# A grouped 1x1 convolution: 64 equal chunks, and seven stores of 120 and 8 rows

## The chip, the core and the metric

The kernel runs on one core of a Trainium2 chip. The metric is the device time of one execution in microseconds (us). Each core has a matrix engine (PE), a vector engine (DVE), a scalar engine (ACT), GpSimd (POOL), an engine that only issues and synchronises (SP), and sixteen DMA engines that carry all traffic between the chip's main memory (DRAM) and the core's two-dimensional memory of 128 rows, called partitions here as in the code.

## What is computed

A 1x1 convolution in 4 groups: each of 512 x 512 pixels has 192 channels, in four groups of 48, and each group is multiplied by its own 48 x 48 matrix. All of it is bf16, with sums in f32.

```python
B, H, W, C = x.shape          # 1, 512, 512, 192
xg = xp.reshape(B, H, W, G, Cg)          # G = 4, Cg = 48, k = 1: no padding
out = out + jnp.einsum('bhwgc,gcd->bhwgd', xg, w[0, 0])
return out.reshape(B, H, W, C)
```

So 262,144 pixels of 384 bytes are read and as many written: 100.7 MB each way.

## The kernel before

**Tiling.** The pixels are cut into chunks. A chunk of s pixels per partition is 128 x s consecutive pixels: partition p holds s of them, a contiguous run of s x 384 bytes in DRAM (`rows_view`, L102). `sizes` (L62) is the list of chunks: five of 4, 4, 8, 16 and 32 pixels (`HEAD`), sixty of 32 (`PPC`), and five of 32, 16, 8, 4 and 4 (`TAIL`), 70 in all. A chunk of 32 is 12,288 bytes a partition and 1.5 MB in all. There are five input buffers `x_sb` and five output buffers `o_sb` (`NB`); chunk n uses number n modulo 5.

**Work in a chunk.** Four pixels per partition make a group, 512 groups in all. For a group PE transposes six 128 x 128 pieces of `x_sb` into `xT_ps` (L181), DVE copies them to `xT_sb` (L235), and PE multiplies them in two rounds of three by a banded weight matrix `wt` into `o_ps` (L204). Two results of 128 x 384 f32 are then cast into `o_sb`: for seven groups in ten by ACT in one copy (L275), for the other three (`SHARE`) one by ACT (L272) and one by DVE (L242). PE's transposes run two groups ahead of its products (`LOOK`).

**Who issues what.** SP issues the loads in order (L149), the small load of the weights just behind the first chunk (L151). From the sixth chunk on, a load waits until PE has transposed the last group of the chunk that used the buffer. ACT issues the stores (L259) between its copies: the store of a chunk when the products of two further groups are done. ACT and DVE wait, before the first write into an output buffer, until the earlier store from it has landed (L242 and the copies at L272 and L275; the semaphores `st_sem`). Each transfer raises its semaphore by 16, by one for each DMA engine that has finished its share.

**PE's program.** `build_weights` (L160 to L169) puts the 48 x 48 matrices into the band by ten products and waits for the weights' load; then come the transposes of the first groups, the groups of `HEAD` one by one, a loop of 12 trips over five chunks of 32 each, and the groups of `TAIL`. Within the loop PE waits by taking from semaphores (`take`), in the tail by counting (`wq.wait`).

Of the kernel before, what the change touches and what calls it, by code (L numbers as in the profile page):

```python
# [11 lines left out]
C = GROUPS * CG  # L12
# [11 lines left out]

PPC = 32
NB = 5
HEAD = (4, 4, 8, 16, 32)
TAIL = (32, 16, 8, 4, 4)
NXP = 4
NOB = 4  # L30
NXS = 4
LOOK = 2
# [16 lines left out]
def shared(g):  # L49
    return (g % 10) in SHARE  # L50


def bass_standalone__grouped__vision_kernel(nc, x, w, out):
# [2 lines left out]
    npix = B * H * W_  # L56
    assert npix % 128 == 0
    per_part = npix // 128
    mid = per_part - sum(HEAD) - sum(TAIL)
    assert mid > 0 and mid % (NB * PPC) == 0  # L60
    n_mid = mid // PPC
    trips = n_mid // NB  # L62
    sizes = list(HEAD) + [PPC] * n_mid + list(TAIL)
    assert len(HEAD) % NB == 0
    n_chunks = len(sizes)

    xf = x.rearrange("b h w c -> (b h w) c")
    of = out.rearrange("b h w c -> (b h w) c")
# [7 lines left out]
    groups, g0 = [], []  # L76
# [2 lines left out]
        groups += [(n, lg) for lg in range(s // 4)]  # L79
    NG = len(groups)  # L80
    g1 = [g0[n] + sizes[n] // 4 for n in range(n_chunks)]
    L0 = g0[len(HEAD)]
    L1 = g0[len(HEAD) + n_mid]
    body = NB * PPC // 4
    assert body % NXP == 0 and body % 10 == 0 and (L1 - L0) == body * trips
    GT = L1

    dve_prog = []
    for g in range(NG + LOOK):
        if g < NG:  # L90
            dve_prog.append(("ev1", g))
        h = g - LOOK
# [3 lines left out]
    def actT_cnt(g):  # L96
        return g - GT + 1

    def dveT_cnt(g):
        return sum(1 for h in range(GT, g + 1) if shared(h))  # L100

    def rows_view(ap, n):  # L102
        s = sizes[n]
        return ap[pix0[n]:pix0[n] + 128 * s, :].rearrange("(p i) c -> p (i c)", p=128)

    with ExitStack() as es:
        block = es.enter_context(nc.Block())
        x_sb = [es.enter_context(nc.sbuf_tensor(f"x_sb{i}", [128, PPC * C], BF16)) for i in range(NB)]
        o_sb = [es.enter_context(nc.sbuf_tensor(f"o_sb{i}", [128, PPC * C], BF16)) for i in range(NB)]
# [8 lines left out]
        def sem(name):  # L118
            return es.enter_context(nc.semaphore(name))

        ld_sem = [sem(f"ld{i}") for i in range(NB)]
        st_sem = [sem(f"st{i}") for i in range(NB)]
# [3 lines left out]
        ev1_sem, ev2_sem, act_sem = sem("ev1_sem"), sem("ev2_sem"), sem("act_sem")  # L126
        ev2T_sem, actT_sem = sem("ev2T_sem"), sem("actT_sem")
# [14 lines left out]
        @block.sync  # L142
        def _(sp):
            wq = Waiter(sp)
            for n in range(n_chunks):
                b = n % NB
                if n >= NB:
                    wq.wait(t_done, g1[n - NB])
                sp.dma_start(x_sb[b][:, 0:sizes[n] * C], rows_view(xf, n)).then_inc(ld_sem[b], 16)  # L149
                if n == 0:  # L150
                    sp.dma_start(w_sb[:], wv).then_inc(w_sem, 16)  # L151

        @block.tensor
        def _(pe):
            wq = Waiter(pe)

            def take(s, v):
                pe.wait_ge(s, v).then_inc(s, -v)  # L158

            def build_weights():  # L160
                wq.wait(e_sem, 1)
                wq.wait(w_sem, 16)
                last = None
                for (tc, r, g, c0) in WBLOCKS:
                    s0 = ESHIFT - r
                    col = WOFF[tc] + c0
                    last = pe.matmul(o_ps[:, NOB - 1, col:col + CG], lhsT=esel[:, s0:s0 + 128],  # L167
                                     rhs=w_sb[:, g, :], start=True, stop=True, skip_group_check=True)
                last.then_inc(wb_sem, 1)  # L169

            def transposes(g):
                n, lg = groups[g]
                b = n % NB
                if g == 0:
                    wq.wait(id_sem, 1)
                if lg == 0:
                    take(ld_sem[b], 16)
                last = None
                for j in range(6):
                    col = lg * 2 * UC + j * 128  # L180
                    last = pe.transpose(xT_ps[:, g % NXP, j * 128:(j + 1) * 128],  # L181
                                        x_sb[b][:, col:col + 128], ident[:])
                last.then_inc(t_done, 1)

            def matmuls(g):
                xs = xT_sb[g % NXS]
                take(ev1_sem, 1)
                h = g - 2
                if h >= 0:
                    if h < GT:  # L190
                        take(act_sem, 1)
                        if shared(h):
                            take(ev2_sem, 1)
                    else:
                        wq.wait(actT_sem, actT_cnt(h))
                        if shared(h):
                            wq.wait(ev2T_sem, dveT_cnt(h))
                last = None
                for ul in range(2):
                    v = (2 * g + ul) % NOB  # L200
                    for tc in range(3):
                        j = ul * 3 + tc
                        c0, c1 = COLR[tc]
                        last = pe.matmul(o_ps[:, v, c0:c1], lhsT=xs[:, j * 128:(j + 1) * 128],  # L204
                                         rhs=wt[:, WOFF[tc]:WOFF[tc] + (c1 - c0)],
                                         start=(tc == 0), stop=(tc == 2), skip_group_check=True)
                last.then_inc(mm_done, 1)

            build_weights()
            for g in range(LOOK):  # L210
                transposes(g)
            pe.wait_ge(wc_sem, 1)
            for g in range(L0):
                transposes(g + LOOK)
                matmuls(g)
            with pe.Fori(0, trips):
                for g in range(L0, L0 + body):
                    transposes(g + LOOK)
                    matmuls(g)
            for g in range(L1, NG):  # L220
                if g + LOOK < NG:
                    transposes(g + LOOK)
                matmuls(g)

        @block.vector
        def _(dve):
            wq = Waiter(dve)
            wq.wait(wb_sem, 1)
            dve.tensor_copy(wt[:], o_ps[:, NOB - 1, 0:WCOLS]).then_inc(wc_sem, 1)  # L229
            waited_chunk = -1  # L230
            for (op, g) in dve_prog:
                n, lg = groups[g]
                if op == "ev1":
                    wq.wait(t_done, g + 1)
                    dve.tensor_copy(xT_sb[g % NXS][:], xT_ps[:, g % NXP, 0:2 * UC]).then_inc(ev1_sem, 1)  # L235
                else:
                    if waited_chunk != n:
                        waited_chunk = n
                        wq.wait(st_sem[n % NB], 16 * (n // NB))
                    wq.wait(mm_done, g + 1)  # L240
                    u = lg * 2 + 1
                    dve.tensor_copy(o_sb[n % NB][:, u * UC:(u + 1) * UC],  # L242
                                    o_ps[:, (2 * g + 1) % NOB, 0:UC]).then_inc(
                                        ev2_sem if g < GT else ev2T_sem, 1)

        @block.scalar
        def _(act):
            wq = Waiter(act)
            pending = []

            def store(n):
                b = n % NB
                g = g1[n] - 1
                if g < GT:
                    wq.wait(mm_done, g + 3)
                else:
                    wq.wait(actT_sem, actT_cnt(g))
                    wq.wait(ev2T_sem, dveT_cnt(g))
                act.dma_start(rows_view(of, n), o_sb[b][:, 0:sizes[n] * C]).then_inc(st_sem[b], 16)  # L259

            for g in range(NG):
                n, lg = groups[g]
                if lg == 0:
                    wq.wait(st_sem[n % NB], 16 * (n // NB))
                wq.wait(mm_done, g + 1)
                while pending and pending[0][1] <= g:
                    store(pending.pop(0)[0])
                v = (2 * g) % NOB
                ob = o_sb[n % NB]
                if shared(g):  # L270
                    u = lg * 2
                    ins = act.copy(ob[:, u * UC:(u + 1) * UC], o_ps[:, v, 0:UC])  # L272
                else:
                    dst = ob[:, lg * 2 * UC:(lg + 1) * 2 * UC].rearrange("p (u c) -> p u c", u=2)
                    ins = act.copy(dst, o_ps[:, v:v + 2, 0:UC])  # L275
                ins.then_inc(act_sem if g < GT else actT_sem, 1)
                if g == g1[n] - 1:
                    pending.append((n, g + 2 if g < GT else g + 1))
            for (n, _) in pending:
                store(n)  # L280
            for b in range(NB):
                act.wait_ge(st_sem[b], 16 * len(range(b, n_chunks, NB)))


# [26 lines left out]
```

## Time and profile before

| what | value |
|---|---|
| runs | 495.13, 495.61, 495.68 us, median 495.61 |
| the profiled execution's own time | 495.92 us |
| its span, first to last instruction | 493.8 us |
| PE clock granted, mean over the span | 0.986 |
| read from and written to DRAM | 100.68 and 100.66 MB, 408 GB/s over the span |
| one ACT copy of 768 columns (L275), of 384 (L272) | 799 ns x 359, 480 ns x 153 |
| one DVE copy of 768 columns (L235), of 384 (L242) | 554 ns x 512, 553 ns x 153 |
| one transposition, one product on PE (L181, L204) | 220 ns x 3072, 233 ns x 3072 |
| first loads of 192 KB, last stores of 192 KB, issue to landing (median) | 11.4, 7.3 us |
| SP's waits for PE's transposes, before loads | 438.7 us in 65 waits |

The profile's page divides the span by engine, DMA queue and line of the program. "Busy" is the time in which an engine carries out an instruction. The queue q1 carries SP's loads, q10 ACT's stores; their share is that of the time of all sixteen DMA engines, over the whole span. A table of stretches gives the same for any part of the span. In the table of waits a row says which engine waited at which line for which, in us, how often and at most how long. Matmuls are pipelined, so PE's mean times overlap.

### The profile page before, as it was taken

The page shows a single profiled execution, that of the slowest core. Times are in us where ns is not written, and L with a number is a line of the kernel's source. Part 1 is how long each engine was busy: PE and PEld are TensorE (multiplying, and loading weights), DVE is VectorE, ACT ScalarE, POOL GpSimd, SP SyncE. Part 2 cuts the span into 40 slices and gives each one's busy share as a digit, 9 for nine tenths or more (in the row PEclk, how much of TensorE's full clock was granted, in tenths as well). Part 3 has the DMA queues.
Part 4 walks back from the last instruction along what each step waited for, and adds up shares of the span by engine and source line. Part 5 has one row for each costly group of instructions (what it writes and reads, how often), then busy time and mean ns, then how long its engine had stood idle before and what let it go on. Part 6 is the DMA issues. An engine that isn't in the chain of part 4 may idle for free. (4 is left out here: it accounts for less than half of the span.)

```text
span 493.8 us, 15051 instructions
## 1 busy us (share of the span) xinstructions
PE 418.9 (85%) x6154; PEld 390.4 (79%) x6154; DVE 348.4 (71%) x666; ACT 349.7 (71%) x513; POOL 1.3 (0%) x8
## 2 busy tenths in 40 slices
PE   6987999999988888888888988888888888888962
PEld 5987899999878787787877877878778787787862
DVE  4776788888877776776776767677667767677750
ACT  3776788888867767677676766766767667676752
POOL 1000000000000000000000000000000000000000
PEclk9999999999999999999999999999999999999995
DMA  8999999999999999999999999999999999999663
GB/s 298 420 419 425 427 429 428 429 429 427 426 429 429 429 428 429 428 429 429 429 429 429 428 429 429 429 429 428 429 428 428 429 429 429 429 428 417 239 254 143
DMA packets 20386, 201.56 MB, mean 408 GB/s; under 512 B 2448, under 2 KB 3472, under 8 KB 4496
## 3 DMA queue, kind: packets, MB, share of 16 engines
q1 hardware_dynamic: 10288, 100.69, 48.4%
q10 hardware_dynamic: 10080, 100.67, 48.2%
q8 instruction: 7, 0.11, 0.1%
q14 instruction: 11, 0.09, 0.0%
HBM read 100.68 MB, written 100.66 MB: 408 GB/s over the span
## 5 line engine op out<-in xcount | busy, mean ns | idle before, releaser
L275 ACT CAST o_sb<-o_ps 128x768 bf16<-128x768 f32 x359 | 280.3, 799 | 103.6 <-PE o_ps L204 66.5
L235 DVE COPY xT_sb<-xT_ps 128x768 bf16<-128x768 bf16 x512 | 282.2, 554 | 97.2 <-PE xT_ps L181 92.6
L204 PE MATMUL o_ps<-wt,xT_sb 128*128 128x144 bf16 (+1 forms) x3072 | 298.0, 233 | 48.7 <-PEq L158 46.7
L181 PE MATMUL xT_ps<-ident,x_sb 128*128 128x128 bf16 x3072 | 257.0, 220 | 16.4 <-PEq L158 12.3
L204 PEld LDWEIGHTS o_ps<-wt,xT_sb 128*128 128x128 bf16 x3072 | 211.4, 98 | 67.0 <-issue 57.7
L181 PEld LDWEIGHTS xT_ps<-ident,x_sb 128*128 128x128 bf16 x3072 | 196.0, 98 | 26.2 <-issue 26.1
L242 DVE CAST o_sb<-o_ps 128x384 bf16<-128x384 f32 x153 | 84.6, 553 | 35.7 <-DMA out_dram<-o_sb 21.5
L272 ACT CAST o_sb<-o_ps 128x384 bf16<-128x384 f32 x153 | 73.4, 480 | 34.9 <-DMA out_dram<-o_sb 21.2
L229 DVE CAST wt<-o_ps 128x480 bf16<-128x480 f32 x1 | 0.7, 657 | 4.2 <-PE o_ps L167 4.2
L167 PE MATMUL o_ps<-w_sb,esel 48*128 48x48 bf16 x10 | 0.6, 209 | 3.6 <-DMA w_sb<-in_w_dram 3.6
L167 PEld LDWEIGHTS o_ps<-w_sb,esel 48*128 48x128 bf16 x10 | 0.5, 111 | 3.5 <-issue 3.5
L275 ACT ACT_TABLE_LOAD x1 | 1.3, 1283 | 0.8 <-PEq L296 0.8
L134 POOL TENSOR_SCALAR_AFFINE_SELECT esel<-esel 48x272 bf16<-48x272 bf16 x1 | 0.4, 406 | 0.0
L131 POOL MEMSET esel<- 48x272 bf16 x1 | 0.3, 318 | 0.3 <-POOLq L296 0.3
L138 POOL TENSOR_SCALAR_AFFINE_SELECT ident<-ident 128x128 bf16<-128x128 bf16 x1 | 0.3, 287 | 0.0
L132 POOL MEMSET ident<- 128x128 bf16 x1 | 0.2, 198 | 0.0
L296 POOL MEMSET const-bfloat16-1.0<- 128x1 bf16 x1 | 0.1, 102 | 0.0
L296 POOL MEMSET const-uint8-127<- 128x1 uint8 x1 | 0.1, 102 | 0.0
L296 POOL MEMSET const-float32-0.0<- 128x1 f32 x1 | 0.1, 99 | 0.3 <-issue 0.3
L296 POOL MEMSET const-float32-1.0<- 128x1 f32 x1 | 0.1, 99 | 0.0
## 6 DMA issues: line engine op xcount, KB each, us to landing
x_sb<-in_x_dram SPq DMA_DIRECT2D x62, 1536.0 KB, 30.9
out_dram<-o_sb ACTq DMA_DIRECT2D x62, 1536.0 KB, 30.5
x_sb<-in_x_dram SPq DMA_DIRECT2D x2, 768.0 KB, 17.8
out_dram<-o_sb ACTq DMA_DIRECT2D x2, 768.0 KB, 13.9
x_sb<-in_x_dram SPq DMA_DIRECT2D x4, 192.0 KB, 11.4
x_sb<-in_x_dram SPq DMA_DIRECT2D x2, 384.0 KB, 15.3
out_dram<-o_sb ACTq DMA_DIRECT2D x4, 192.0 KB, 7.3
out_dram<-o_sb ACTq DMA_DIRECT2D x2, 384.0 KB, 10.8
```

The source lines that it names most:

```text
L131: gp.memset(esel[:], 1.0).then_inc(p0_sem, 1)
L134: gp.affine_select(out=esel[:], in_=esel[:], pattern=[[-1, ECOLS]], compare_op=AluOpType.is_equal, fill=0.0, base=ESHIFT, channel_multipli ...
L138: gp.affine_select(out=ident[:], in_=ident[:], pattern=[[-1, 128]], compare_op=AluOpType.is_equal, fill=0.0, base=0, channel_multiplier=1) ...
L167: last = pe.matmul(o_ps[:, NOB - 1, col:col + CG], lhsT=esel[:, s0:s0 + 128], rhs=w_sb[:, g, :], start=True, stop=True, skip_group_check=True)
L181: last = pe.transpose(xT_ps[:, g % NXP, j * 128:(j + 1) * 128], x_sb[b][:, col:col + 128], ident[:])
L204: last = pe.matmul(o_ps[:, v, c0:c1], lhsT=xs[:, j * 128:(j + 1) * 128], rhs=wt[:, WOFF[tc]:WOFF[tc] + (c1 - c0)], start=(tc == 0), stop=( ...
L229: dve.tensor_copy(wt[:], o_ps[:, NOB - 1, 0:WCOLS]).then_inc(wc_sem, 1)
L235: dve.tensor_copy(xT_sb[g % NXS][:], xT_ps[:, g % NXP, 0:2 * UC]).then_inc(ev1_sem, 1)
L242: dve.tensor_copy(o_sb[n % NB][:, u * UC:(u + 1) * UC], o_ps[:, (2 * g + 1) % NOB, 0:UC]).then_inc(ev2_sem if g < GT else ev2T_sem, 1)
L272: ins = act.copy(ob[:, u * UC:(u + 1) * UC], o_ps[:, v, 0:UC])
L275: ins = act.copy(dst, o_ps[:, v:v + 2, 0:UC])
L296: nc = _bacc.Bacc("TRN2", target_bir_lowering=False, num_devices=1)
```

## The change

The head and the tail of small chunks go: all 64 chunks have 32 pixels per partition. Sixty of them are PE's loop, which now begins with the first group; the last four (`TAIL`) are written out behind it. Because the loop's groups take from `act_sem` from the first one on, ACT raises that semaphore by 2 at its start. The stores of the chunks 8, 16, 24, 32, 40, 48 and 56 (`RELIEF`) are each issued as two transfers: rows 0 to 119 and rows 120 to 127. The counts that the reuse of an output buffer waits for (`st_before`) follow.

```diff
-HEAD = (4, 4, 8, 16, 32)
-TAIL = (32, 16, 8, 4, 4)
+TAIL = (32, 32, 32, 32)
+RELIEF = tuple(range(8, 60, 8))
+RELIEF_ROWS = ((0, 120), (120, 128))
...
-    mid = per_part - sum(HEAD) - sum(TAIL)
+    mid = per_part - sum(TAIL)
...
-    sizes = list(HEAD) + [PPC] * n_mid + list(TAIL)
-    assert len(HEAD) % NB == 0
+    sizes = [PPC] * n_mid + list(TAIL)
...
+    def store_parts(n):
+        return RELIEF_ROWS if n in RELIEF else ((0, 128),)
+
+    st_total, acc = [], [0] * NB
+    for n in range(n_chunks):
+        acc[n % NB] += 16 * len(store_parts(n))
+        st_total.append(acc[n % NB])
+
+    def st_before(n):
+        return st_total[n - NB] if n >= NB else 0
...
-                if h >= 0:
-                    if h < GT:
-                        take(act_sem, 1)
-                        if shared(h):
-                            take(ev2_sem, 1)
...
+                if h < GT:
+                    take(act_sem, 1)
+                    if shared(h):
+                        take(ev2_sem, 1)
...
-            for g in range(L0):
-                transposes(g + LOOK)
-                matmuls(g)
             with pe.Fori(0, trips):
-                for g in range(L0, L0 + body):
+                for g in range(body):
                     transposes(g + LOOK)
                     matmuls(g)
...
-                        wq.wait(st_sem[n % NB], 16 * (n // NB))
+                        wq.wait(st_sem[n % NB], st_before(n))
...
             wq = Waiter(act)
+            act.sem_inc(act_sem, 2)
             pending = []
...
-                act.dma_start(rows_view(of, n), o_sb[b][:, 0:sizes[n] * C]).then_inc(st_sem[b], 16)
+                dst = rows_view(of, n)
+                for (r0, r1) in store_parts(n):
+                    act.dma_start(dst[r0:r1, :], o_sb[b][r0:r1, 0:sizes[n] * C]).then_inc(st_sem[b], 16)
...
-                act.wait_ge(st_sem[b], 16 * len(range(b, n_chunks, NB)))
+                act.wait_ge(st_sem[b], acc[b])
```

More of the change, by code (lines that the diff above doesn't have):

```diff
@@ L81, in bass_standalone__grouped__vision_kernel @@
     g1 = [g0[n] + sizes[n] // 4 for n in range(n_chunks)]
-    L0 = g0[len(HEAD)]
-    L1 = g0[len(HEAD) + n_mid]
+    L1 = g0[n_mid]
     body = NB * PPC // 4
-    assert body % NXP == 0 and body % 10 == 0 and (L1 - L0) == body * trips
+    assert body % NXP == 0 and body % 10 == 0 and L1 == body * trips
+    assert not shared(-1) and not shared(-2)
     GT = L1
@@ L188, in matmuls @@
                 h = g - 2
-                if h >= 0:
-                    if h < GT:
-                        take(act_sem, 1)
-                        if shared(h):
-                            take(ev2_sem, 1)
[L194 to L197, printed above, removed]
+                if h < GT:
+                    take(act_sem, 1)
+                    if shared(h):
+                        take(ev2_sem, 1)
+                else:
+                    wq.wait(actT_sem, actT_cnt(h))
+                    if shared(h):
+                        wq.wait(ev2T_sem, dveT_cnt(h))
                 last = None
@@ L263, in _ @@
                 if lg == 0:
-                    wq.wait(st_sem[n % NB], 16 * (n // NB))
+                    wq.wait(st_sem[n % NB], st_before(n))
                 wq.wait(mm_done, g + 1)
```

## The prediction

> **What bounds the kernel now.** I read the page first, then the stretches of the span, then the waits, then the times at which each transfer's sixteen shares land. The page: no compute engine fills the span, the two DMA queues together do.
>
> ```profile
> PE 418.9 (85%) x6154; PEld 390.4 (79%) x6154; DVE 348.4 (71%) x666; ACT 349.7 (71%) x513; POOL 1.3 (0%) x8
> ...
> q1 hardware_dynamic: 10288, 100.69, 48.4%
> q10 hardware_dynamic: 10080, 100.67, 48.2%
> ...
> x_sb<-in_x_dram SPq DMA_DIRECT2D x62, 1536.0 KB, 30.9
> out_dram<-o_sb ACTq DMA_DIRECT2D x62, 1536.0 KB, 30.5
> ```
>
> 48.4% + 48.2% is 96.6% of sixteen engines' time. A chunk of 32 pixels takes 30.9 us from issue to landing, over four times the 7.3 us between chunks, so several loads and stores are always queued. The stretches (busy time of each engine, granted clock, DMA share, GB/s) show where the missing part lies:
>
> ```profile
> 0.00:5.00 5.00, 1.31 (x16) 1.01 (x16) 0.74 (x2) 1.28 (x1) 1.31 (x8) 1.00 0.58 153
> 5.00:10.00 5.00, 4.69 (x47) 4.29 (x48) 2.60 (x5) 1.60 (x2) 0.00 (x0) 1.00 0.98 384
> 10.00:15.00 5.00, 4.76 (x70) 4.18 (x68) 4.06 (x9) 3.62 (x6) 0.00 (x0) 1.00 1.01 417
> 15.00:20.00 5.00, 4.78 (x76) 4.56 (x74) 3.85 (x9) 4.02 (x7) 0.00 (x0) 1.00 0.99 409
> ...
> 200.00:250.00 50.00, 42.21 (x630) 39.41 (x627) 35.45 (x68) 35.41 (x53) 0.00 (x0) 1.00 1.01 428
> ...
> 455.00:460.00 5.00, 4.85 (x76) 4.49 (x73) 4.31 (x9) 3.49 (x6) 0.00 (x0) 1.00 0.78 313
> 460.00:465.00 5.00, 3.93 (x60) 3.57 (x58) 3.21 (x7) 3.79 (x6) 0.00 (x0) 1.00 0.74 306
> 465.00:470.00 5.00, 4.98 (x79) 4.67 (x76) 4.32 (x9) 4.00 (x7) 0.00 (x0) 1.00 0.50 188
> ...
> 480.00:485.00 5.00, 2.38 (x21) 2.06 (x20) 0.65 (x2) 0.80 (x1) 0.00 (x0) 0.50 0.43 174
> 485.00:490.00 5.00, 2.45 (x17) 1.75 (x15) 0.46 (x1) 2.40 (x3) 0.00 (x0) 0.50 0.35 137
> ```
>
> The middle runs at 428 GB/s with a share of 1.01. The last 40 us do not: the share falls to 0.35, and PE sits at half clock, waiting. It is not the work that has run out, as the landings show. A transfer raises its semaphore sixteen times, once per DMA engine, and the trace has each time. For loads, the first landing and by how much the 14th, 15th and 16th come later (us):
>
> ```
> load of chunk   first     14th  15th  16th
> 10               42.42     1.8   2.4   2.6
> 20              115.56     2.4   2.6   5.1
> 40              261.88     2.6   3.6  11.6
> 60              408.19     4.1   4.1  18.1
> 63              430.13     4.0   4.8  19.2
> ```
>
> Fifteen engines keep within 5 us of each other; one falls back steadily, 18.1 - 5.1 = 13.0 us in 40 chunks, 0.325 us a chunk. The stores have the same tail (store of chunk 60: fifteenth 4.7 us after the first, sixteenth 19.4). The fast ones take (408.19 - 115.56) / 40 = 7.316 us for a chunk's load and store, 0.457 us for each of their 16 rows of 12,288 bytes; the lagging one 7.641 us, 0.478 us a row. All have the same eight rows of every transfer. Since a transfer counts as landed at its sixteenth share, that one engine sets the end, and the waits agree: everyone waits a little for the chunk that is not complete.
>
> ```profile
> DVE xT_sb L235 <- PE xT_ps L181: 92.6, 261, 3.7
> ...
> ACT o_sb L275 <- DMA out_dram<-o_sb: 32.4, 27, 1.4
> ```
>
> As a check, the lagging engine's bill: 2048 pixels are 64 chunks' worth, 64 x 7.641 = 489.0 us. Its first packet starts at 1.8 us. In the first 20 us the core moved 5 x (153 + 384 + 417 + 409) = 6,815 KB where 18.2 us at 428 GB/s are 7,790 KB: 2.3 us lost at the head. From the last landing (493.3) to the end of the span 0.5. Sum 493.6 against the 493.8 profiled. The bill closes, so I use it for the change.
>
> **The split stores.** Seven of 64 chunks store rows 0 to 119 and rows 120 to 127 by two transfers. Nothing in the trace has 120 or 8 rows, so how they are shared out is bounded. From the row of 128: 8 rows to each of 16. 120 is 15 such shares; if it goes out so, one engine is left out. At the other end, 120 rows spread so that every engine gets its part again (relief 0), or onto fewer engines (a loss, priced below). I take 15 shares, the nearest to the row seen, with the eight single rows on eight of the engines.
> The Trainium skill ("DMA: Bandwidth & Descriptors", section "Why a DMA increments its semaphore by 16 and not by 1") says the number of engines is the largest up to 16 that divides the rows, on the lowest-numbered ones: 15 for 120, 8 for 8. No run here shows that yet; by it the spared engine is number 15 and engines 0 to 7 get a row more, which is the split I take, so the sum is the same.
> The spared engine then loses 7 x 8 = 56 rows: 56 x 0.478 = 26.7 us, and its bill is 489.0 - 26.7 = 462.3. Seven engines stay at 64 x 7.316 = 468.2, and the eight with one row more per split are at 468.2 + 7 x 0.457 = 471.4. Relief comes every eight chunks, in which the lag grows by only 8 x 0.325 = 2.6 us and is cut by 3.8, so it never builds up. If the lagging engine is the spared one, the eight become the longest.
> To that come the lags among the fast fifteen, 0 to 4.8 us at the end of the trace, which have nothing to do with the split; twelve are within 2.6 and I take that.
>
> **Equal chunks at the head.** The loads go from 0.2 MB first to 1.5 MB first: chunk 0 needs 8 x 0.457 = 3.7 us and lands near 6 us instead of at 3.3, and the weights behind it on SP's queue come with it instead of at 3.4. So PE, and behind it DVE and ACT, start 2.5 to 3 us later. What hides it: five loads are issued at once, 5 x 3.66 = 18.3 us of DMA work, busy until 20 us. The sixth waits for chunk 0's last transpose; in the old trace the first eight groups' transposes took 7.5 us (4.06 to 11.57), so it is released at about 13.7, 6 us ahead of need. Were that cover gone, the head would pay the 2.5 us. The gain: rows of 1,536 bytes take 65 ns there, 23.6 GB/s for one engine against 26.9 with 12,288 bytes, and they go. The head loss is between 0.3 and the old 2.3; I take 0.7.
>
> **Equal chunks at the tail.** The last store is 1.5 MB instead of 0.2 MB. The first store waits for the products of ten groups: 6.2 (landing) + 3.1 (weights to first product in the old trace, 3.57 to 6.70) + 9.4 (ten groups there, 6.70 to 16.05) = 18.7 us. By then loads have moved (18.7 - 2.5) / 3.66 = 4.4 chunks, and two queues that share each engine equally keep that lead. So when the last load lands, 4.4 chunks of stores, 16 us, are still to move, and the last chunk's compute (8 groups at 0.77 us, 4 us of landing spread, 1.3 us of start: 11.5 us) is done before the 3.4 chunks ahead of it, 12.4 us, have gone. Cost nothing; with a lead of three chunks it would be 11.5 + 3.7 - 11.0 = 4.2 us.
>
> **ACT, PE, SP.** Loads fall from 70 to 64; stores go from 70 to 64 + 7. Seven more issues on ACT at 0.34 us are 2.4 us, behind which the next copy of o_ps waits, and PE for that bank; ACT is idle for over 130 us of the span, so nothing. Its reuse wait now asks for both parts of a split store. PE needs some 0.77 us a group, 394 us for 512, far below the DMA's 471. The two early increments of act_sem cost nothing.
>
> **Sum.** 471.4 + 2.6 (lag) + 1.8 (first packet) + 0.7 (head) + 0.5 (end) = 477.0 us of span. The profiled run took 495.92 for a span of 493.8, 2.1 more, and the median (495.61) is 0.3 below it: 477.0 + 1.8 = 478.8. I say 479. With lag and head at their ends: 472.0 + 2.3 = 474.3 plus 1.8, 476, to 471.4 + 4.8 + 1.8 + 2.3 + 0.5 + 1.8 = 482.6; a tail that comes bare takes it to 486.
>
> **Rivals.**
> *The lagging engine is one of those that get a row more.* The trace does not number the engines. Then its bill is 489.0 + 7 x 0.478 = 492.3, and with 1.8 + 0.7 + 0.5 + 1.8 the time is 497.1, slower by 0.3%. It decides as soon as the lagging engine is among the eight: the whole relief goes to an engine that is not late.
> The skill's page on DMA (section "Latency and other measured facts") says that engines 7 and 15 are usually slower, and guesses a cause on GpSimd's path, which this kernel doesn't use for DMA; the trace has one late engine, not two. By 7 the sum is this rival's 497.1, by 15 the forecast's 479.
> *It is one that neither gains nor loses,* or the 120 rows leave nobody out: 489.0 + 1.8 + 0.7 + 0.5 + 1.8 = 493.8, faster by 0.4% through the head alone, or the same if the head loss stays.
> *120 rows go out over eight engines,* 15 to each: 8 rows more with the single one, 7 x 8 x 0.457 = 25.6: 468.2 + 25.6 + 2.6 + 1.8 + 0.7 + 0.5 + 1.8 = 501.2. For it: only 128 rows are seen to spread over 16. Against: the 48 rows of the weights landed by sixteen increments too.
> *Fifteen shares, but slower,* since rows no longer lie as the engines have them: from 0 to, at half rate, 7 x 3.66 = 25.6 us, 479 to 505.
>
> **How the numbers follow.** Which engine is late is a judgement: one that differs from fifteen alike sits more likely at an end of the row than inside it, and of the ends one is spared. I put 0.76 on the forecast (476 to 486), 0.07 on slower shares that eat a part of it (486 to 494), 0.05 on no relief (493.8, of it 0.02 the same), 0.06 on the late engine getting more (497.1), 0.06 on eight engines or shares at half rate (above 500). One measurement of this kernel tells 0.2%, 1 us, from no change. Faster: 0.76 + 0.07 + 0.03 = 0.86; same 0.02; slower 0.12. The range 474.5 to 489 leaves out the last three and half of the second; the forecast's own is 476 to 486.
>
> **What would show it.** In the new trace the sixteenth landing should trail the fifteenth by no more than some 4 us all along, falling by about 3.8 after each split; the DMA share should stay near 1.0 to about 465 us; 1,440 KB and 96 KB stores, seven of each; PE at full clock to the last chunk. A lag that still grows by 0.325 us a chunk shows the wrong engine spared; a group of engines falling back at each split shows the 120 rows on fewer; a bare gap between the last load and the last store shows the tail uncovered.

## The result, and the profile after

The changed kernel takes 503.23 us (median; 502.37 to 504.17) where the kernel before took 495.64 in the same session: a ratio of 1.016, with a 95% interval of 1.0141 to 1.0178. It is slower by 7.6 us; 479 was forecast, with faster at 0.86. The profiled execution took 502.37 us and spans 500.5. Times here and below are medians of all executions of a run; the ratios leave out the few that were over 1.5% above the fastest of the same kernel.

The page of the changed kernel, engines, queues, the chain that ended last and the DMA issues:

```profile
PE 414.0 (83%) x6154; PEld 396.1 (79%) x6154; DVE 347.5 (69%) x666; ACT 348.8 (70%) x513; POOL 1.3 (0%) x8
...
q1 hardware_dynamic: 9424, 100.69, 48.5%
q10 hardware_dynamic: 9265, 100.67, 48.2%
...
DMA 68%; PE 3%; ACT 2%; ACTq 0%; issue 0%
...
x_sb<-in_x_dram SPq DMA_DIRECT2D x64, 1536.0 KB, 22.5
out_dram<-o_sb ACTq DMA_DIRECT2D x57, 1536.0 KB
out_dram<-o_sb ACTq DMA_DIRECT2D x7, 1440.0 KB
out_dram<-o_sb ACTq DMA_DIRECT2D x7, 96.0 KB
```

The engines are busy for as long as before. The chain is now made of stores for 68% of the span: work waits for output buffers. The packets of q10 tell how the stores went out. 8,192 rows need 8,192 packets; the rest, 9,265 - 8,192 = 1,073, are the completions, one for each engine of each transfer: 57 whole stores x 16 = 912 leaves 161, 23 for each split store, 15 for the 120 rows and 8 for the eight. So the split is the one that the prediction took. The rule of the Trainium skill ("DMA: Bandwidth & Descriptors", section "Why a DMA increments its semaphore by 16 and not by 1"), the largest count up to 16 that divides the rows, agrees with these counts.

The stretches (busy time of each engine, granted clock, DMA share, GB/s):

```profile
0.00:5.00 5.00, 0.00 (x0) 0.00 (x0) 0.00 (x0) 1.28 (x1) 1.31 (x8) 1.00 0.58 216
5.00:10.00 5.00, 2.56 (x30) 2.52 (x31) 1.77 (x3) 0.00 (x0) 0.00 (x0) 1.00 1.03 426
10.00:15.00 5.00, 5.00 (x65) 4.89 (x63) 3.44 (x7) 3.21 (x5) 0.00 (x0) 1.00 1.01 425
...
200.00:250.00 50.00, 42.00 (x613) 40.15 (x612) 33.97 (x66) 33.78 (x51) 0.00 (x0) 0.97 1.01 426
250.00:300.00 50.00, 39.33 (x576) 37.76 (x576) 32.63 (x63) 32.98 (x49) 0.00 (x0) 0.97 1.01 421
300.00:350.00 50.00, 39.25 (x597) 37.68 (x598) 33.96 (x67) 34.06 (x51) 0.00 (x0) 1.00 1.01 417
350.00:400.00 50.00, 43.48 (x640) 41.71 (x638) 36.13 (x70) 35.83 (x53) 0.00 (x0) 0.97 1.00 401
400.00:430.00 30.00, 24.88 (x357) 23.90 (x355) 20.18 (x39) 19.96 (x31) 0.00 (x0) 0.94 0.99 405
...
465.00:470.00 5.00, 4.71 (x75) 4.71 (x76) 3.81 (x8) 4.46 (x8) 0.00 (x0) 1.00 0.83 335
470.00:475.00 5.00, 2.09 (x34) 1.92 (x32) 1.85 (x4) 1.62 (x3) 0.00 (x0) 1.00 0.33 138
...
495.00:500.00 5.00, 0.00 (x0) 0.00 (x0) 0.00 (x0) 0.00 (x0) 0.00 (x0) 0.50 0.40 170
```

The kernel before has in one of these stretches:

```profile
350.00:400.00 50.00, 42.52 (x630) 39.55 (x630) 35.33 (x68) 35.18 (x53) 0.00 (x0) 1.00 1.01 428
```

The head is better than before (216 and 426 GB/s for 153 and 384). From 250 us on there is something new: the DMA share stays at 1.00, but fewer bytes move, 421, then 417, then only 401 GB/s where 428 did. The DMA engines are busy and slower. At the end the share still falls, to 0.33 and 0.40, as work waits for one late engine.

The waits of ACT and DVE for stores were, at DVE's copy and ACT's small one (the large one had 32.4 us):

```profile
DVE o_sb L242 <- DMA out_dram<-o_sb: 21.5, 26, 1.2
ACT o_sb L272 <- DMA out_dram<-o_sb: 21.2, 18, 1.2
```

They grew to:

```profile
ACT o_sb L285 <- DMA out_dram<-o_sb: 42.5, 23, 5.2
DVE o_sb L249 <- DMA out_dram<-o_sb: 29.6, 20, 4.4
ACT o_sb L282 <- DMA out_dram<-o_sb: 23.7, 14, 2.9
```

The landings show whom the split served. Each line is one of the last four split stores of the changed kernel: its first data landing (the two increments before it, at once on issue, are those of the issuing side), the twelfth of the 23, and how much later the last four come (us):

```
store of chunk   first data   12th later   last four later
32                 265.83        4.7       7.5   8.1  17.2  18.6
40                 322.75        4.7      11.6  11.6  23.6  25.0
48                 384.80        3.6       9.7  10.6  24.4  25.8
56                 447.31        2.7       6.7   7.3  24.7  25.8
```

The last two stand alone, far behind the rest and 1.1 to 1.4 us apart. They read as two shares of the same late engine, one of the 120 rows and one of the eight. So it was not spared: it is one of the eight that got a row more. Runs 4, 7 and 8 test this reading.

### The profile page after: what moved, and what is told of

It reads as the page before. It is cut to its first block, busy times and chain, and to the rows that moved or that the text cites. A ratio compares the mean times of both kernels' runs of the same rounds, so it can differ in the third digit from the quotient of the medians.

```text
span 500.5 us, 15020 instructions
## 1 busy us (share of the span) xinstructions
PE 414.0 (83%) x6154; PEld 396.1 (79%) x6154; DVE 347.5 (69%) x666; ACT 348.8 (70%) x513; POOL 1.3 (0%) x8
## 3 DMA queue, kind: packets, MB, share of 16 engines
q10 hardware_dynamic: 9265, 100.67, 48.2%
## 4 chain that ended last, share of the span: by engine, by line
DMA 68%; PE 3%; ACT 2%; ACTq 0%; issue 0%
DMA out_dram<-o_sb 68%; PE o_ps L214 2%; ACT o_sb L285 2%; PE xT_ps L192 1%; ACTq L269 0%; ACT o_sb L282 0%; ACTq L47 0%
## 5 line engine op out<-in xcount | busy, mean ns | idle before, releaser
L192 PEld LDWEIGHTS xT_ps<-ident,x_sb 128*128 128x128 bf16 x3072 | 200.2, 99 | 2.2 <-issue 2.0
```

## The experiments

All are edits of the changed kernel except the second. The kernel before, run beside them, stood between 495.07 and 495.47. Runs 1 to 7 ran on one chip, 8 to 10, 11 and 12, and 13 to 15 on three others.

**1. No split.** The store of every chunk goes out whole.

```diff
-RELIEF = tuple(range(8, 60, 8))
+RELIEF = ()
```

> 64 equal chunks, no store split. Theory A (the late DMA engine is one of the first eight and each split hands it a row more and slows it by about 1 us besides): the splits' cost goes, the time is 493 to 496 us, at or just below the 495.6 of before. Theory B (the missing ramps at head and tail cost the 7.6 us): 500 to 503 us.

493.01 us, a ratio of 0.9951 (0.9932 to 0.997). Equal chunks are faster by 0.5%; the splits cost 503.2 - 493.0 = 10.2 us. Theory B falls. No wait for a store is left in its table of waits, while PE still waits for loads (in `take`, L169) and the others for PE:

```profile
DVE xT_sb L242 <- PE xT_ps L192: 111.1, 266, 1.4
ACT o_sb L285 <- PE o_ps L214: 94.0, 171, 8.6
...
PE xT_ps L192 <- PEq L169: 41.5, 46, 1.1
```

Its late engine keeps a steady 7.63 us a chunk in loads and stores. That is the scale for the runs below.

**2. The splits alone**, in the kernel before with its ramps.

```diff
+RELIEF = tuple(range(8, 60, 8))
+RELIEF_ROWS = ((0, 120), (120, 128))
...
-                act.dma_start(rows_view(of, n), o_sb[b][:, 0:sizes[n] * C]).then_inc(st_sem[b], 16)
+                dst = rows_view(of, n)
+                for (r0, r1) in store_parts(n):
+                    act.dma_start(dst[r0:r1, :], o_sb[b][r0:r1, 0:sizes[n] * C]).then_inc(st_sem[b], 16)
```

> The kernel before with its small first and last chunks, and the seven stores split into 120 and 8 rows. Theory A: 495.6 + 7 x (0.48 + 1) = 506 us at most, 503 at least. Theory B: 495.6 plus the seven extra rows alone, 496 to 499 us.

507.68 us, 1.0244 (1.0202 to 1.0287). The splits cost 12.3 us here, a little above what theory A allowed. With run 1 this shows that the loss is in the splits and not in the missing ramps.

**3. 112 and 16 rows.** Both parts use all sixteen engines; no engine carries more.

```diff
-RELIEF_ROWS = ((0, 120), (120, 128))
+RELIEF_ROWS = ((0, 112), (112, 128))
```

> 64 equal chunks, seven stores split into 112 and 16 rows: by the rule seen in the counts both parts go to all sixteen engines (7 rows and 1 row each), so no engine's load changes. Theory A: as without a split, 493 to 496 us. Rival C (a second transfer in a store costs by itself, through its issue on ACT or its second set of completions): near the 503 us of the changed kernel.

500.94 us, 1.0105 (1.0088 to 1.0123): 7.9 us above run 1, though no engine's load changed. Theory A as stated falls: a split costs something apart from the extra rows. Rival C stood, for the moment.

**4. Which engine is late.**

```diff
-RELIEF = tuple(range(8, 60, 8))
-RELIEF_ROWS = ((0, 120), (120, 128))
+RELIEF = {20 + 4 * r: ((0, 112), (112, 128 - r), (128 - r, 128)) for r in range(1, 8)}
```

> A probe for the number of the late engine: the stores of the chunks 24, 28, .. 48 go out as 112 rows, 16 - r rows and r rows, r = 1 to 7; a part of k rows (k up to 16) is expected on the k lowest engines. The late engine lands a share of the last part only when its number is below r. If the late engine is number j below eight, the last landings of the store (those some 10 us or more behind the rest) are two for r up to j and three from r = j + 1 on. If it is number 7, all seven stores show two late landings. The time should be near that of the changed kernel, 497 to 508 us.

506.15 us in a single execution. The last four landings of the probed stores, in us behind the first increment:

```
chunk   r   the last four landings
24      1   24.1  24.8  28.5  29.9
28      2   23.7  23.9  28.8  30.1
32      3   23.7  24.9  29.7  31.1
36      4   23.2  24.9  32.6  34.0
40      5   16.5  28.1  29.2  30.5
44      6   19.5  30.2  31.7  33.0
48      7   14.9  28.8  30.2  31.6
```

Two late shares up to r = 4, three from r = 5 on: a part of four rows misses the late engine, and one of five reaches it. With the parts on the lowest engines, as the expectation takes it, the late engine is number 4, the fifth of sixteen. The Trainium skill ("DMA: Bandwidth & Descriptors", section "Latency and other measured facts") says that engines 7 and 15 are usually slower, with a guessed cause on GpSimd's path, which this kernel does not use; the measurement differs, and decides here.

**5. Two transfers, same rows.** The split goes through the columns.

```diff
-RELIEF_ROWS = ((0, 120), (120, 128))
+HALVES = ((0, PPC // 2 * C), (PPC // 2 * C, PPC * C))
...
-                for (r0, r1) in store_parts(n):
-                    act.dma_start(dst[r0:r1, :], o_sb[b][r0:r1, 0:sizes[n] * C]).then_inc(st_sem[b], 16)
+                for (c0, c1) in store_parts(n):
+                    act.dma_start(dst[:, c0:c1], o_sb[b][:, c0:c1]).then_inc(st_sem[b], 16)
```

> 64 equal chunks; the seven stores are split by columns, all 128 rows with the first 16 pixels and then all 128 rows with the last 16. Two transfers, and every engine keeps its own eight rows. Theory A2 (a split costs because its rows are shared out otherwise, so that engines get in each other's way): no cost, 492 to 495 us as without a split. Theory C (the second transfer itself costs about 1.1 us): 499 to 503 us.

495.99 us, 1.0011 (1.0001 to 1.0022): 3.0 us above run 1, between the two theories and nearer to A2. The last share of a split store landed 11.2 to 11.4 us after that of the store before it, at six of the seven splits, where 7.63 is usual. Both figures fit an engine that takes a load packet and a store packet in turn: 16 store packets of 6,144 bytes (234 ns) with a load packet of 12,288 (460 ns) beside each make 16 x 0.694 = 11.1 us; eight large ones make 8 x 0.92 = 7.4. So smaller packets, not the second transfer as such, make the store late; that the 3.0 us come from this was not tested by itself.

**6. 64 and 64 rows.**

```diff
-RELIEF_ROWS = ((0, 120), (120, 128))
+RELIEF_ROWS = ((0, 64), (64, 128))
```

> 64 equal chunks; the seven stores are split into rows 0 to 63 and 64 to 127, four rows of each for every engine. No engine's load changes, the rows that an engine carries do. Theory A2: like the split of 112 and 16, 498 to 503 us. Theory C: the same, so this run tells them apart only together with the split by columns; if both are at 493, the cost lies in parts of unequal size.

504.07 us, 1.0196 (1.0142 to 1.0251): 8.1 us above the split by columns, with the same number of transfers, the same bytes on each engine and larger packets. What is left to differ is which rows an engine carries. That part of the cost belongs to the sharing by rows; theory C cannot make it. The traces do not name the rows of an engine.

**7. 120, 4 and 4 rows: nothing more on engine 4.**

```diff
-RELIEF_ROWS = ((0, 120), (120, 128))
+RELIEF_ROWS = ((0, 120), (120, 124), (124, 128))
```

> 64 equal chunks; the seven stores are split into 120, 4 and 4 rows: the last eight rows go to the engines 0 to 3, two to each, and the late engine, number 4 by the probe, gets no row more. If the extra rows on the late engine cost their 7 x 0.48 = 3.3 us, the time is about 500 us against the 503.2 of 120 and 8. If the number of transfers is what costs, it is 503 us or more.

496.56 us, 1.0039 (1.0008 to 1.007), with single runs from 494.3 to 501.8. One transfer more than the changed kernel, and 6.7 us less.

**8. 120, 5 and 3 rows: one row more on engine 4.**

```diff
-RELIEF_ROWS = ((0, 120), (120, 128))
+RELIEF_ROWS = ((0, 120), (120, 125), (125, 128))
```

> 64 equal chunks; seven stores split into 120, 5 and 3 rows. Against 120, 4 and 4 one thing changes: the part of five rows reaches the engine 4, which the probe shows as the late one. If the extra row on the late engine alone costs, the time is 496.6 + 7 x 0.48 = 500 us. If the whole difference between 120 and 8 (503.2) and 120, 4 and 4 (496.6) comes with that row, 503 us. If the extra rows on that engine don't matter, 496 to 497 us.

499.89 us, 1.0104 (1.0082 to 1.0126), 3.3 us above run 7, as the seven rows at 0.478 us would have it. The ratios leave some 2 us either way in that difference, and longer packets have a part in it (below).

**9 and 10. Real relief for engine 4, and the opposite.** The second half of three chunks' columns goes to the engines 0 to 3 alone, or to the engines 0 to 4.

```diff
-RELIEF = tuple(range(8, 60, 8))
-RELIEF_ROWS = ((0, 120), (120, 128))
+RELIEF = (16, 32, 48)
+HALF = PPC // 2 * C
+PARTS = ((0, 128, 0, HALF), (0, 124, HALF, 2 * HALF), (124, 128, HALF, 2 * HALF))
```

In run 10, 125 stands in place of 124.

> 64 equal chunks; the stores of chunks 16, 32 and 48 go out as the first 16 pixels of all rows on sixteen engines, and the last 16 pixels as 124 and 4 rows, which go to the engines 0 to 3 alone. The late engine 4 loses 3 x 4 = 12 rows' worth (5.7 us), the engines 0 to 3 take 36 more (16.5 us), which still leaves them ahead of it. If engine 4's own load sets the end: 493.0 - 5.7 + some 1.5 for six more transfers = 487 to 491 us. If not: 493 us or, where the loaded engines set it, more.

> As the run before, but the last 16 pixels go out as 125 and 3 rows; 125 rows go to five engines, 25 each, engine 4 among them. It gains 3 x (12.5 - 4) = 25.5 rows' worth, 12.2 us. If engine 4 sets the end: 493.0 + 12.2 + 1.5 = 505 to 508 us, some 17 us above the run before, though the engines 0 to 3 have less to do. If it does not: no more than the run before.

Run 9: 498.08 us, 1.0063 (1.0048 to 1.0078). Run 10: 507.48, 1.0254 (1.0238 to 1.0269). The second lies in its range, but 9.4 us above run 9 where some 17 were expected; the first misses. The relief itself arrived: the last load's sixteenth share trailed the first by 4.3 us, where it was 21.7 in run 1. But it brought no time, and the waits of run 9 show what came in its place, a few very long waits for an output buffer:

```profile
ACT o_sb L286 <- DMA out_dram<-o_sb: 35.8, 6, 15.4
DVE o_sb L250 <- DMA out_dram<-o_sb: 31.7, 5, 15.7
```

Run 10 has such waits too, so that its loss is engine 4's load or the long burst, or both:

```profile
ACT o_sb L286 <- DMA out_dram<-o_sb: 42.4, 14, 14.2
```

Run 9's stretches show a DMA that runs short of work in the middle of a run:

```profile
200.00:250.00 50.00, 48.28 (x731) 45.98 (x729) 41.07 (x80) 40.72 (x60) 0.00 (x0) 1.00 1.01 428
250.00:300.00 50.00, 31.68 (x447) 30.48 (x445) 24.80 (x49) 25.98 (x38) 0.00 (x0) 0.83 0.91 382
```

The split store of chunk 16 ended some 20 us after most of its shares had landed; its buffer came free that much later, and PE stood still (31.68 us busy of 50).

**11 and 12. The same relief in smaller bursts.** Eight pixels in each of six chunks, or four in each of twelve.

```diff
-RELIEF = (16, 32, 48)
-HALF = PPC // 2 * C
+RELIEF = tuple(range(8, 56, 8))
+MOST = 24 * C
...
```

Run 12 has `range(4, 52, 4)` and `28 * C`.

> As the run with 124 and 4 rows on the engines 0 to 3, but 8 pixels in each of six chunks (8, 16, .. 48) in place of 16 in each of three: the same 12 rows' worth less on engine 4, in bursts half as long (32 x 3,072 bytes an engine, 3.7 us at most, against 7.3). If the long bursts were what held output buffers and cost that run its relief: 493.0 - 5.7 + 6 x 2 x 0.43 for the transfers = 492 us or less. If the transfers or the sharing cost it: 496 to 500 us.

> The same relief in twelve chunks (4, 8, .. 48), 4 pixels each: bursts of 1.8 us, 24 more transfers. By the burst account 487 to 493 us; if each transfer costs 0.43 us, 493.0 - 5.7 + 10.3 = 498 us.

498.87 us, 1.0083 (1.0064 to 1.0101), and 501.11, 1.0127 (1.0108 to 1.0146). A miss for the burst account: the bursts became half and a quarter as long in bytes, and nothing was won. Run 11 lies in the range named for a cost of the transfers or the sharing, run 12 above the 498 named for the transfers. The packet count of run 5 may explain it, as an argument and not as a separate test: each of the four engines still has 32 packets to send, each behind a load packet of 460 ns. With rows of 6,144, 3,072 and 1,536 bytes (234, 121 and 65 ns) that is 22, 19 and 17 us. In run 11 the split stores still ended 33 us after their first increment (chunks 16 and 40), where run 9 had 40 and 43 (chunks 16, and 32 and 48). By this account the burst was long in packets, not in bytes.

**13. The 120 rows alone.** Rows 120 to 127 of seven chunks are not stored.

```diff
-RELIEF_ROWS = ((0, 120), (120, 128))
+RELIEF_ROWS = ((0, 120),)
```

> 64 equal chunks; in the seven stores only the rows 0 to 119 are stored, and rows 120 to 127 are left out. One transfer, engine 15 without a share, all others as in a whole store. If the 120 rows on fifteen engines are free and the cost is in the part of eight rows: 492 to 494 us, as without a split. If the part of fifteen shares costs: 496 us (the level of 120, 4 and 4) to 500 us.

500.38 us, 1.0082 (1.0053 to 1.011), with single runs from 495.0 to 503.3. Fewer bytes, no second transfer, no row more on engine 4, and yet slower than whole stores by 7 us. The spared engine runs ahead: in its trace the sixteen shares of a load lay within 0.6 us of each other at chunk 1, and at chunk 31 one came 12.3 us before the next and 26.1 before the last. Its waits for stores are short, 23.2 us in all where the kernel before has 75.1, so that such waits are not what makes this kernel slow:

```profile
ACT o_sb L285 <- DMA out_dram<-o_sb: 12.4, 20, 2.3
ACT o_sb L282 <- DMA out_dram<-o_sb: 7.0, 16, 2.0
DVE o_sb L249 <- DMA out_dram<-o_sb: 3.8, 3, 1.9
```

**14. The small part in front.**

```diff
-RELIEF_ROWS = ((0, 120), (120, 128))
+RELIEF_ROWS = ((0, 8), (8, 128))
```

> [...] If it costs that engines carry other rows than usual: 505 us or more. If the loads alone count: 503 us, as the changed kernel.

505.83 us, 1.0208 (1.0179 to 1.0237), 2.6 us above the changed kernel, its single runs from 503.5 to 508.9. By the counting rule each engine has as many rows as in the changed kernel, and only the order of the parts differs. It leans towards the account by rows, and is too near to 503 to settle it.

**15. 112 rows alone.** Rows 112 to 127 of seven chunks are not stored.

```diff
-RELIEF_ROWS = ((0, 120), (120, 128))
+RELIEF_ROWS = ((0, 112),)
```

> 64 equal chunks; in the seven stores only the rows 0 to 111 are stored, rows 112 to 127 are left out. One transfer, seven rows for each engine, mostly not those of a whole store. Each engine has 7 rows less, the late one 3.3 us. If other rows cost nothing: 493.0 - 3.3 = 490 us. If they cost what 112 and 16 cost (8 us): 495 to 498 us.

494.37 us, 0.9968 (0.9942 to 0.9994), single runs from 489.8 to 497.4: some 4 us more than the 490 that the bytes alone would give, just below what was named. So something costs here too, without a second transfer and without a spared engine; that it is the other rows is not shown.

**What the slower runs have in common.** Nearly all store packets of 12,288 bytes take 460 ns. The table counts those that took over 520 ns in the profiled execution of each kernel, among stores and among loads, and what the stores among them took beyond 460 ns in sum. Its last column is the mean packet of the late engine. A packet's record names no engine, but on one engine each packet starts 3 or 4 ns before the one ahead of it ends, and each share ends with a 4-byte completion, so the packets can be strung into sixteen chains. That is an estimate: where two engines end within a nanosecond or two, they can be taken for each other. Between 20 and 430 us one chain takes 481 to 493 ns a packet and pauses for 0.6 us at most, in every kernel listed with a value. A spared engine's chain can be as slow, but pauses for 2 to 7 us and has fewer stores.

```
stores                         span us   over 520 ns      excess us   late engine's
                                         stores  loads    of stores   mean, ns
112 alone (run 15)              491.0      66      96        30         483.9
whole (run 1)                   492.0       7      74         3         480.9
120, 4, 4 (run 7)               492.5      65     150        25         481.8
columns (run 5)                 494.2      35     252         7            -
120, 5, 3 (run 8)               497.7     138     207        50         482.9
120 alone (run 13)              500.2     222     184        89         491
120, 8 (the changed kernel)     500.5     177     287        67         485.7
112, 16 (run 3)                 500.9     166     217        82         491.3
64, 64 (run 6)                  501.3     171     208        83         490.6
120, 8, with ramps (run 2)      505.2     247     320        90         489.5
8, 120 (run 14)                 507.1     284     353       110         493.1
```

Single packets of the changed kernel reach 1.7 us among stores and 1.9 among loads. The long ones among stores come in clusters while a split store is under way; among loads, apart from the first 40 us, nearly all come from 320 us on. This is the slower DMA of the stretches above: busy, at 401 GB/s. The count rises with the span only roughly, and it does not by itself give the time: the columns have as many long loads as the slow kernels, and the runs 9 to 12 have only 26 to 45 long stores at 498 to 507 us.

The late engine's own packets do give it. Its chain in the changed kernel has 519 large store packets, seven above the 512 of whole stores. Seven rows at 0.478 us are 3.3 us; packets longer by 4.8 ns than in run 1 are, over 1,031 of them, 4.9 us. The sum is 8.2, and the two spans differ by 8.5. The same estimate gives 5.4 for run 8 (5.7 measured), 0.9 for run 7 (0.5), 10.7 for run 3 (8.9), 10.0 for run 6 (9.3), 10 for run 13 (8.2), 15.9 for run 14 (15.1) and, with seven rows fewer, -0.3 for run 15 (-1.0). So a split by rows costs by what it adds to the late engine, rows and longer packets. What those packets wait for is not seen in these traces.

No version beat equal chunks with whole stores: 493.0 us is 0.5% below the kernel before and 2% below the changed one.

## Why the prediction was wrong

*What bounds the kernel* was read rightly. One DMA engine of sixteen takes 4.4% longer for every row (0.478 us for 0.457) and sets the end. Its bill held for equal chunks: the sum for a change that gives no relief was 493.8, and run 1 measured 493.0. A row more on it cost what the bill says, as far as run 8 against run 7 can tell (3.3 us for seven, give or take 2).

*The head and the tail* went as worked out: the first store was issued at 18.43 us against 18.7, PE's first product came at 7.4 us against the "near 6 us", which stayed hidden, and the DMA moved 216 and 426 GB/s in the first ten microseconds. Large last stores cost nothing: run 1's end fits the bill.

*The shares* were right: fifteen and eight.

*The step that failed* is the sentence "one that differs from fifteen alike sits more likely at an end of the row than inside it, and of the ends one is spared". It was a judgement with nothing from the trace behind it, and 0.76 of the chance hung on it. The late engine is number 4 by the probe. The spared engine was not the late one, and engine 4 got a row more in each split. That alone takes the prediction's own sum from 479 to 497.1. (Two of its other sums are off by less than 1 us and change nothing: the low end is 471.7 + 2.3, and a bare tail takes the high one to 486.8.)

*The rival* that said so had the mechanism and the sign, at 497.1, and 0.06 of the chance. Its size was short by 6.1 us, because it priced the extra row alone. The missing term stood among the rivals as "fifteen shares, but slower", from 0 to 25.6 us, as if it could not come together with the others. It does: of the 10.2 us between whole and split stores the seven rows are 3.3 by the bill, which leaves 6.9. That rest is the dearer part, and it needs no extra row: 112 and 16 rows pay 7.9 us, 64 and 64 pay 11.1. It is not the fifteen shares that set the end, as that rival had it, but the late engine's packets, which took 485.7 ns for 480.9.

*The signs* named a still growing lag for the wrong engine spared. It came in another form. The spared engine ran ahead: the first share of a load was 1.1 us before the second at chunk 20 and 9.5 at chunk 31. The lag of the sixteenth behind the fifteenth was 1.0 us at chunk 20 and 7.2 at chunk 40, while the whole spread grew from 6.3 to 17.2 us. Two late shares in the later split stores said it most plainly.

*What stays open*: what the long packets wait for, whether it comes from the rows that an engine carries or from engines out of step, and how the 6.9 us divide between the 120 rows and the eight. The runs with the 120 rows (500.4 alone, 496.6 with 4 and 4) contradict any simple sum, and their single runs scatter over 7 to 8 us. Whether relief of engine 4 can pay was tried only in forms with many small packets on few engines.

## What to carry to other kernels

Before relieving the one slow unit among many, find out which it is: a transfer whose shares reach only the first k engines, for several k, tells in a single run where the late one stands. Where an engine serves a load and a store packet in turn, as the 11.2 us of run 5 fit, many small store packets hold an output buffer long, however few bytes they are. And splitting a store by rows has a price of its own here, 7.9 to 11.1 us for seven stores with no row more on any engine, which a plan for relief has to count.

## What the runs showed of the hardware that was not expected

One DMA engine takes some 0.478 us for a row of 12,288 bytes where fifteen take 0.457, and falls 20 us behind in one execution; in the probe it is number 4, and the chains of run 8 and of runs 13 to 15, on two other chips, have such an engine too. It is not slow by itself: in run 1 its last ten packets, after all others had ended, took 460 ns each. Engines can be fully busy at 401 GB/s in place of 428, with single packets of up to 1.9 us in place of 0.46, after some stores were split by rows. And leaving bytes out can cost time: seven stores without their last eight rows took 7 us longer than whole ones.
